# Long convolution with a gate: the first three transform stages on quarter blocks of the PE array

## The chip, the cores and the metric

One core of a Trainium2 chip. The metric is the device time of one execution in microseconds. Five engines are named as the profile names them: PE (the matmul array; PEld is its weight load), DVE (VectorE), ACT (ScalarE), POOL (GpSimd) and SP (SyncE, which issues the DMAs here). PSUM holds matmul results in banks of 512 fp32 columns on 128 partitions. All data are fp32.

## The reference, cut to what matters

```
x: (8, 6400, 128)   h: (6400, 128)                  # batch, time, channel
y = irfft(rfft(x, 12800) * rfft(h, 12800))[:, :6400]  # causal long convolution
gate = sigmoid(sum_k conv_w[k] * shift(y, 4 - k))     # 5 taps, causal
out = (gate * (y @ w_val)) @ w_out
```

## The kernel before, in words

The convolution is a shifted discrete Fourier transform of 6400 = 100 x 64 points, done as matmuls in four stages for one batch of 128 channels at a time. `n1`, `k1` run over 100 (`N1`), `n2`, `k2` over 64 (`N2`).

- Stage 1 (`Forward.group`, tile `x` or `h` to `gy` or `gh`): the weights loaded into the array are the data, 100 rows (`n1`) by 128 columns (two channels by 64 `n2`); the moving operand is the table `r1_sb` of 100 x 200 (cosines, sines). Four calls make a group of 8 channels, and 16 groups (`NG`) a batch. Four copies of 64 partitions x 400 columns bring a group from PSUM to `gy`, real part on partitions 0 to 63, imaginary on 64 to 127.
- Stage 2 (`s2_mm`): for each of the 100 `k1` one call with a 128 x 128 table (`m2_sb`) as weights and 128 channels moving, 8 values of `k1` to a step `kb`, 13 steps (`NKB`). `Product` multiplies by the spectrum of `h`: `swap` (ACT) copies the result from PSUM into `w` with the halves of the partitions exchanged, `mul_u` and `mul_t` (DVE) multiply, `add` (POOL) adds into `gy`. The spectrum is kept in DRAM (`hd`) as two tiles a step, each with its 64 rows doubled, and is loaded for every batch (`h_load`).
- Stage 3 (`s3_quad`): per channel one call, weights from `gy` (128 rows, 100 columns), the table `r3_sb` (128 x 128) moving; four channels fill a bank, which one copy of 100 x 512 brings to `dt`.
- Stage 4 (`Chunk.s4`): weights from `dt` (100 rows, 128 columns), the table `m4_sb` (100 x 100) moving, two calls for each of 64 time offsets. Then taps, projection, sigmoid, gate, output projection and store, in 13 chunks.

At the start the spectrum of `h` and the first batch are transformed. Then every batch has two phases. In phase A (`for g in range(NG)`) stage 3 of this batch runs beside stage 1 of the next one. In phase B (`for s in range(NCH)`) stage 4 and the gate of this batch run beside stage 2 and the product of the next. The last batch has no next one. In the profile phase A is for example 364 to 417 us and phase B 417 to 490 us. Every engine executes in the order in which the code is written (`_InOrder`). A PSUM `pair` is two banks, and two pairs take turns in the main loop; four single banks (`ps1`) serve stages 3 and 4.

Of the kernel before, what the change touches and what calls it, by code (L numbers as in the profile page):

```python
# [19 lines left out]
PX = 112  # L20
KB = 8
# [3 lines left out]
NG = C // XG  # L25
NW = 2 * C + TAPS
SW = 256
# [7 lines left out]
LATER = 5  # L35
M2B = 4
WB = 3
HB = 4
XB = 4
# [11 lines left out]
def _constants():  # L51
    k1 = np.arange(N1, dtype=np.float64)
    n1 = np.arange(N1, dtype=np.float64)
    k2 = np.arange(N2, dtype=np.float64)
    n2 = np.arange(N2, dtype=np.float64)
    tau = 2.0 * np.pi
    a = tau * np.outer(n1, k1 + 0.25) / N1
    r1 = np.concatenate([np.cos(a), -np.sin(a)], axis=1)
    al = tau * (
        (k1[None, :, None] + 0.25) * n2[:, None, None] / N  # L60
        + np.outer(n2, k2)[:, None, :] / N2
    )
    m2 = np.zeros((2, N2, N1, 2 * N2))
    m2[0, :, :, :N2] = np.cos(al)
    m2[1, :, :, :N2] = np.sin(al)
    m2[0, :, :, N2:] = -np.sin(al)
    m2[1, :, :, N2:] = np.cos(al)
    b = tau * np.outer(k2, n2) / N2
    r3 = np.zeros((2 * N2, N2, 2))
    r3[:N2, :, 0] = np.cos(b)  # L70
    r3[N2:, :, 0] = -np.sin(b)
    r3[:N2, :, 1] = -np.sin(b)
    r3[N2:, :, 1] = -np.cos(b)
    t = N2 * n1[None, :] + n2[:, None]
# [28 lines left out]
def longconv_moe(ctx: ExitStack, tc: tile.TileContext, x, h, r1, m2, r3, m4, w64, out):  # L103
# [98 lines left out]
    class Forward:  # L202


        def __init__(self, src, dst):
            self.src, self.dst, self.n, self.i = src, dst, 0, 0

        def load(self, n=1):
            for _ in range(n):
                if self.n < NG:  # L210
                    nc.sync.dma_start(x_sb[self.n % XB], self.src[self.n])
                    self.n += 1

        def group(self):
            g = self.i
            self.i += 1
            t = x_sb[g % XB]
            pt = pair()
            for m in range(4):
                nc.tensor.matmul(  # L220
                    pt[:, m // 2, (m % 2) * SW : (m % 2) * SW + 2 * N1],
                    lhsT=t[:N1, 2 * m : 2 * m + 2, :].rearrange("p j n -> p (j n)"),
                    rhs=r1_sb,
                    start=True,
                    stop=True,
                )
            self.load()
            v = pt.rearrange("p b (m x) -> p b x m", x=SW)
            return [
                lambda e, j=j, c=c: e(  # L230
                    self.dst[c * N2 : (c + 1) * N2, 4 * g + 2 * j : 4 * g + 2 * j + 2],
                    v[j * N2 : (j + 1) * N2, :, c * N1 : (c + 1) * N1],
                )
                for j in range(2)
                for c in range(2)
            ]

    def count(kb):
        return min(KB, N1 - kb * KB)

    def m2_load(kb):
        if kb < NKB:
            n = count(kb)
            nc.sync.dma_start(m2_sb[kb % M2B][:, :n], m2[:, kb * KB : kb * KB + n])

    def h_load(kb):
        if kb < NKB:
            n = count(kb) * C
            for r in range(2):
                nc.sync.dma_start(h_sb[(2 * kb + r) % HB][:, :n], hd[kb, r, :, :n])  # L250

    def h_double(kb):
        n = count(kb) * C
        for r in range(2):
            nc.sync.dma_start(hd[kb, r, N2:, :n], hd[kb, r, :N2, :n])

    def kdt(t, kb):
        n = count(kb)
        return t[:, : n * C].rearrange("p (d k t) -> p d k t", k=n, t=2)

    def s2_mm(src, kb):
        pt = pair()
        n = count(kb)
        for k in range(n):
            nc.tensor.matmul(
                pt[:, k // 4, (k % 4) * C : (k % 4 + 1) * C],
                lhsT=m2_sb[kb % M2B][:, k, :],
                rhs=src[:, :, kb * KB + k],
                start=True,
                stop=True,  # L270
            )
        if n <= 4:
            return pt[:, 0, : n * C].rearrange("p (k d t) -> p d k t", t=2, d=C // 2)
        return pt.rearrange("p b (k d t) -> p d (b k) t", t=2, d=C // 2)

    hx = h_sb + [dt[:, N1 * C + i * KB * C : N1 * C + (i + 1) * KB * C] for i in range(2)]

    class Spectrum:
        def __init__(self, kb):
            self.kb, self.v = kb, s2_mm(gh, kb)  # L280
            self.h = [hx[(2 * kb + r) % len(hx)] for r in range(2)]

        def real(self):
            t = kdt(self.h[0], self.kb)
            act(t[:N2], self.v[:N2])
# [392 lines left out]
```

## Time and profile before

| | |
|---|---|
| three runs | 1084.45, 1085.63, 1087.29 us (median 1085.63) |
| profiled execution, first to last instruction | 1083.8 us; a time of its own is not given beside this span |
| PE, PEld busy | 1048.2 us, 940.6 us |
| DVE, ACT, POOL busy | 848.5, 726.3, 407.5 us |
| DMA | 221.13 MB, mean 204 GB/s |

In the rows of groups "pt<-r_sb,x" is stage 1, "pt<-gy,m" stage 2, "pt<-r_sb,gy" stage 3, "pt<-m_sb,dt" stage 4; "128*100" are rows and columns of the loaded weights, then the output's partitions x columns and the moving operand's. All instructions carry the line of a helper, so tiles tell them apart. One matmul call of the program is recorded as two weight loads and two matmuls (two passes): stage 1 has 576 calls and 1152 of each. The profile's matmul durations include the way through the array, so they overlap.

### The profile page before, as it was taken

How to read it: one execution, taken by the hardware profiler on the slowest of the kernel's cores; microseconds unless marked ns; L12 is line 12 of the kernel's file. 1: busy time of each engine (PE TensorE's matmuls, PEld its weight loads, DVE VectorE, ACT ScalarE, POOL GpSimd, SP SyncE). 2: the span in 40 equal slices, each digit the busy share in tenths (PEclk: the TensorE clock that was granted, in tenths of full speed). 3: DMA queues.
4: the chain of work that ended last, by engine and by line, in shares of the span. 5: the costliest groups of instructions: out<-in, count | busy, mean ns of one | idle time of the engine just before them, and what ended most of it. 6: DMA issues, size and time to landing. Idle time of an engine off the chain costs nothing.

```text
span 1083.8 us, 19535 instructions
## 1 busy us (share of the span) xinstructions
PE 1048.2 (97%) x7480; PEld 940.6 (87%) x7480; DVE 848.5 (78%) x1180; ACT 726.3 (67%) x1176; POOL 407.5 (38%) x216
## 2 busy tenths in 40 slices
PE   8997899999999999999999999999999999999997
PEld 8997899779988899879998799888998789987975
DVE  5789778987599857987589866998579885998375
ACT  5799348865588556875488545984578645885365
POOL 0079005840078102870058400881028600683032
PEclk9999899999999999999999999999999999999999
DMA  5688957974199734977179742997249761892012
GB/s 149 216 305 202 363 181 257 305 227 166 53 336 274 263 94 145 333 214 243 53 271 309 232 151 67 333 280 255 77 172 322 215 228 51 291 309 78 18 38 84
DMA packets 109130, 221.13 MB, mean 204 GB/s; under 512 B 45354, under 2 KB 53518, under 8 KB 108814
## 3 DMA queue, kind: packets, MB, share of 16 engines
q1 hardware_dynamic: 109038, 219.89, 62.9%
q8 instruction: 59, 0.97, 0.4%
q14 instruction: 33, 0.27, 0.1%
HBM read 184.47 MB, written 39.32 MB: 206 GB/s over the span
## 4 chain that ended last, share of the span: by engine, by line
PE 79%; DVE 7%; ACT 6%; DMA 4%; issue 2%; POOL 1%; POOLq 0%; SPq 0%; DVEq 0%; ACTq 0%
PE pt L90 79%; DVE gl L90 2%; ACT w L90 2%; DVE w L90 2%; ACT dt L90 2%; DVE gy L90 2%; DMA x<-xl 1%; DMA h<-hd 1%; DMA m<-m 1%; ACT p L90 1%; DVE dt L90 1%; ACT gl L90 0%; DMA out<-yl 0%; ACT yl L90 0%; POOL gy L90 0%
## 5 line engine op out<-in xcount | busy, mean ns | idle before, releaser
L90 PEld LDWEIGHTS pt<-m_sb,dt 100*128 100x128 f32 x2048 | 242.4, 192 | 43.5 <-issue 30.1
L90 PEld LDWEIGHTS pt<-r_sb,gy 128*100 128x100 f32 x2048 | 239.6, 172 | 28.3 <-issue 24.6
L90 ACT COPY dt<-pt 100x512 f32<-100x512 f32 (+3 forms) x280 | 163.4, 584 | 137.0 <-PE pt L90 135.5
L90 PE MATMUL pt<-r_sb,gy 128*100 128x128 f32 x2048 | 244.7, 274 | 7.0 <-DVE gy L90 7.0
L90 POOL TENSOR_TENSOR gy<-gy,w 128x1024 f32<-128x1024 f32 x95 | 225.8, 2376 | 60.0 <-DVE w L90 59.4
L90 PE MATMUL pt<-m_sb,dt 100*128 100x100 f32 x2048 | 243.7, 274 | 3.5 <-DVE dt L90 2.6
L90 PE MATMUL pt<-r_sb,x 100*128 100x200 f32 x1152 | 216.4, 335 | 5.3 <-DMA x<-hl 4.3
L90 PEld LDWEIGHTS pt<-gy,m 128*128 128x128 f32 x1600 | 194.4, 188 | 24.0 <-issue 10.3
L90 DVE COPY dt<-pt 100x512 f32<-100x512 f32 (+2 forms) x165 | 112.2, 683 | 119.8 <-PE pt L90 117.9
L90 PE MATMUL pt<-gy,m 128*128 128x128 f32 x1600 | 201.7, 279 | 2.8 <-DVE dt L90 2.4
L90 PEld LDWEIGHTS pt<-r_sb,x 100*128 100x128 f32 x1152 | 193.1, 192 | 5.9 <-issue 5.3
L90 ACT COPY gy<-pt 64x400 f32<-64x400 f32 x256 | 124.6, 487 | 100.9 <-PE pt L90 88.6
L90 DVE COPY gy<-pt 64x400 f32<-64x400 f32 x256 | 146.4, 572 | 36.1 <-PE pt L90 33.5
L90 POOL MEMSET dt<- 128x4 f32 x8 | 0.8, 106 | 458.0 <-PE pt L90 458.0
L90 DVE TENSOR_TENSOR w<-w,h 128x1024 f32<-128x1024 f32 (+1 forms) x100 | 148.5, 1485 | 0.0
L90 DVE SCALAR_TENSOR_TENSOR dt<-pt,w_sb,dt 128x500 f32<-128x500 f32 (+7 forms) x216 | 132.5, 629 | 11.5 <-POOL dt L90 6.1
L90 ACT ACTIVATE w<-pt 64x1024 f32<-64x1024 f32 (+1 forms) x104 | 102.8, 989 | 38.3 <-PE pt L90 36.4
L90 DVE TENSOR_TENSOR gy<-pt,h 128x1024 f32<-128x1024 f32 (+1 forms) x100 | 117.5, 1175 | 12.1 <-ACT w L90 6.5
L90 POOL TENSOR_TENSOR dt<-dt,p 128x500 f32<-128x500 f32 (+1 forms) x64 | 101.5, 1586 | 58.0 <-DVE dt L90 34.9
L90 PE MATMUL pt<-dt,w_sb 128*128 128x500 f32 (+2 forms) x240 | 113.8, 564 | 2.3 <-ACT dt L90 2.3
L90 DVE SCALAR_TENSOR_TENSOR gl<-pt,w_sb,gl 128x500 f32<-128x500 f32 (+3 forms) x119 | 73.9, 622 | 38.9 <-ACT gl L90 29.8
L90 ACT COPY w<-pt 64x1024 f32<-64x1024 f32 (+1 forms) x104 | 101.1, 972 | 1.5
(35 smaller groups left out, 722.2 us busy)
## 6 DMA issues: line engine op xcount, KB each, us to landing
h<-hd SPq DMA_DIRECT2D x168, 512.0 KB, 6.8
m<-m SPq DMA_DIRECT2D x96, 512.0 KB, 6.5
x<-xl SPq DMA_DIRECT2D x128, 224.0 KB, 3.4
out<-dt SPq DMA_DIRECT2D x56, 250.0 KB, 6.0
out<-yl SPq DMA_DIRECT2D x40, 250.0 KB, 2.9
hd<-h SPq DMA_DIRECT2D x8, 512.0 KB, 5.7
x<-hl SPq DMA_DIRECT2D x16, 224.0 KB, 2.6
hd<-hd SPq DMA_DIRECT2D x14, 256.0 KB, 4.8
```

The lines of the kernel that those rows point to most:

```text
L90: return self._tc.keep_in_program_order(call(*args, **kwargs))
```

## The change

Stage 1 first folds the 100 values of `n1` in half: `sums` forms the sum (DVE) and the difference (POOL) of a row and its mirror image, 50 rows each, for 16 channels at a time. `half` multiplies these by tables of 50 x 100. Stages 1 and 3 then call the array in blocks of 64 rows x 64 columns, four calls on the four blocks in turn; stage 2 in blocks of 128 rows x 64 columns, two in turn. Calls rise from 3740 to 11240: stage 1 from 576 to 2304, stage 2 from 900 to 3600, stage 3 from 1024 to 4096. Stage 4 keeps its 1024 calls, with 128 rows of weights instead of 100.

In stage 2 the real part stands in one PSUM bank and the imaginary in the next, on all 128 partitions, so `swap` falls away: `mul_u` and `mul_t` read PSUM, each as two operations of 128 x 512, and `add` is two of 128 x 512. The spectrum needs one tile a step instead of two. Copies out of stage 1 go from four of 64 x 400 per 8 channels to two of 128 x 400. Loads of `x` go from 16 of 224 KB to 8 of 512 KB a batch, into two buffers (`XB`) instead of four; at the start six more buffers lie in `m4_sb`.

PE in phase A before, one group of eight channels and the start of the next (pt: PSUM tile, r_sb: table, gy and x: weights; rows are output partitions x columns, x4 means four calls):

```order
L90 MATMUL pt_1755<-r_sb,gy 100x128 x4
L90 MATMUL pt_1760<-r_sb,gy 100x128 x4
L90 MATMUL pt_1765<-r_sb,x_87 128x200 x4
L90 MATMUL pt_1784<-r_sb,gy 100x128 x4
L90 MATMUL pt_1789<-r_sb,gy 100x128 x4
```

and the same place now, from the end of stage 3 for eight channels into stage 1 (r_sb,x and r_sb,d alternate sixteen times, six shown):

```order
L96 MATMUL pt_3684<-r_sb,gy 64x128 x2
L96 MATMUL pt_3685<-r_sb,gy 64x128 x2
L96 MATMUL pt_3684<-r_sb,gy 50x128 x2
L96 MATMUL pt_3685<-r_sb,gy 50x128 x2
L96 MATMUL pt_3718<-r_sb,x_87 64x100
L96 MATMUL pt_3718<-r_sb,d_89 64x100
L96 MATMUL pt_3718<-r_sb,x_87 64x100
L96 MATMUL pt_3718<-r_sb,d_89 64x100
L96 MATMUL pt_3718<-r_sb,x_87 64x100
L96 MATMUL pt_3718<-r_sb,d_89 64x100
```

Eight plus four calls have become 32 plus 16, and two banks of stage 3 are filled at the same time.

DVE in phase B before, two steps (gy<-pt,h is `mul_u`, w<-w,h is `mul_t`, dt<-pt,w_sb,dt the taps, dt<-pt,dt the gate):

```order
L90 TENSOR_TENSOR gy<-pt_2258,h_83 128x64x16
L90 SCALAR_TENSOR_TENSOR dt<-pt_2270,w_sb,dt 128x5x100 x3
L90 TENSOR_TENSOR w_92<-w_92,h_84 128x1024
L90 TENSOR_TENSOR dt<-pt_2309,dt 128x5x100
L90 TENSOR_TENSOR gy<-pt_2299,h_85 128x64x16
L90 SCALAR_TENSOR_TENSOR dt<-pt_2311,w_sb,dt 128x5x100 x3
L90 TENSOR_TENSOR w_93<-w_93,h_86 128x1024
```

and now:

```order
L96 TENSOR_TENSOR gy<-pt_6416,h_84 128x64x8 x2
L96 SCALAR_TENSOR_TENSOR dt<-pt_6452,w_sb,dt 128x5x100 x3
L96 TENSOR_TENSOR w_91<-pt_6416,h_84 128x512 x2
L96 TENSOR_TENSOR dt<-pt_6515,dt 128x5x100
L96 TENSOR_TENSOR gy<-pt_6481,h_85 128x64x8 x2
L96 SCALAR_TENSOR_TENSOR dt<-pt_6517,w_sb,dt 128x5x100 x3
L96 TENSOR_TENSOR w_92<-pt_6481,h_85 128x512 x2
```

`mul_t` now reads the PSUM tile too, behind the taps, so the pair comes free there and no longer with `mul_u` and ACT's copies.

The diff, cut to its core (the tables of constants, the layout of `x` and `h` and the declarations of tiles that only follow from it are left out):

```diff
-XB = 4
+XB = 2
-HB = 4
+HB = 3
...
-        def group(self):
-            g = self.i
+        def sums(self):
+            j = self.i // 2
+            x, d = self.xs[j % len(self.xs)], d_sb[j % 2]
+            nc.gpsimd.tensor_tensor(out=d, in0=x[:, 0], in1=x[:, 1], op=ALU.subtract)
+            nc.vector.tensor_tensor(out=x[:, 0], in0=x[:, 0], in1=x[:, 1], op=ADD)
+
+        def half(self):
+            j, q = self.i // 2, self.i % 2
             self.i += 1
-            t = x_sb[g % XB]
+            x, d = self.xs[j % len(self.xs)], d_sb[j % 2]
             pt = pair()
             for m in range(4):
-                nc.tensor.matmul(
-                    pt[:, m // 2, (m % 2) * SW : (m % 2) * SW + 2 * N1],
-                    lhsT=t[:N1, 2 * m : 2 * m + 2, :].rearrange("p j n -> p (j n)"),
-                    rhs=r1_sb,
...
-            self.load()
+                for r, c in ((0, 0), (1, 1), (1, 0), (0, 1)):
+                    rows = slice(r * HP, r * HP + HR)
+                    nc.tensor.matmul(
+                        pt[c * N2 : (c + 1) * N2, r, m * N1 : (m + 1) * N1],
+                        lhsT=(d if c else x[:, 0])[rows, 4 * q + m, :],
+                        rhs=r1_sb[rows, c, :],
...
+            if q:
+                self.load()
...
     def s2_mm(src, kb):
...
-        for k in range(n):
-            nc.tensor.matmul(
-                pt[:, k // 4, (k % 4) * C : (k % 4 + 1) * C],
-                lhsT=m2_sb[kb % M2B][:, k, :],
-                rhs=src[:, :, kb * KB + k],
+        for s in range(n):
+            for c in range(2):
+                for p, k in ((0, 0), (1, 0), (1, 1), (0, 1)):
+                    o = (p + k) % 2
+                    nc.tensor.matmul(
+                        v[o * N2 : (o + 1) * N2, c, k * C // 4 : (k + 1) * C // 4, s, :],
+                        lhsT=m2_sb[kb % M2B][:, s, p, c * N2 : (c + 1) * N2],
+                        rhs=src[:, k * C // 4 : (k + 1) * C // 4, p * HR + kb * SB + s, :],
...
-        def swap(self):
-            nc.scalar.activation(self.t[:N2], self.v[N2:], AF.Copy, scale=-1.0)
-            act(self.t[N2:], self.v[:N2])
         def mul_u(self):
-            nc.vector.tensor_tensor(out=self.u, in0=self.v, in1=self.h[0], op=MUL)
+            for c in range(2):
+                nc.vector.tensor_tensor(out=self.u[:, c], in0=self.v[:, c], in1=self.h[:, 0], op=MUL)
         def mul_t(self):
-            nc.vector.tensor_tensor(out=self.t, in0=self.t, in1=self.h[1], op=MUL)
+            for c in range(2):
+                nc.vector.tensor_tensor(out=self.t[:, c], in0=self.v[:, c], in1=self.h[:, 1], op=MUL)
...
+        def add(self, e=nc.gpsimd):
+            for c, op in ((0, ALU.subtract), (1, ADD)):
+                e.tensor_tensor(out=self.u[:, c], in0=self.u[:, c], in1=self.t[:, 1 - c], op=op)
...
+    def s3_quads(d0):
+        pts = [single(), single()]
         for q in range(4):
-            d = d0 + q
-            nc.tensor.matmul(
-                pt[:N1, q * 2 * N2 : (q + 1) * 2 * N2],
-                lhsT=gy[:, d // 2, :, d % 2],
-                rhs=r3_sb,
+            for c in range(2):
+                for r, k in ((0, 0), (1, 0), (1, 1), (0, 1)):
+                    d, o = k * HP + d0 + q, (r + k) % 2
+                    m = HR if c else HP
+                    nc.tensor.matmul(
+                        pts[k][o * HP : o * HP + m, q * 2 * N2 : (q + 1) * 2 * N2],
+                        lhsT=gy[r * HP : (r + 1) * HP, d // 2, c * HR : c * HR + m, d % 2],
+                        rhs=r3_sb[r * HP : (r + 1) * HP, c, :],
+                        start=c == 0,
+                        stop=c == 1,
...
+        for g in range(NQ):
+            if nxt and g % 2 == 0:
+                fx.sums()
+            e = s3_quads(4 * g)
+            f = fx.half() if nxt else []
             e[0](act)
             e[1](dve)
-            for i in f:
-                i(act if g % 2 else dve)
+            if nxt:
+                f[0](act)
+                f[1](dve)
```

More of the change, by code (lines that the diff above doesn't have):

```diff
@@ L55, in _constants @@
     n2 = np.arange(N2, dtype=np.float64)
+    half = np.arange(2 * HP) % HP
+    own = half < HR
     tau = 2.0 * np.pi
-    a = tau * np.outer(n1, k1 + 0.25) / N1
-    r1 = np.concatenate([np.cos(a), -np.sin(a)], axis=1)
+    a = tau * np.outer(half + 0.5, k1 + 0.25) / N1
+    r1 = np.stack([np.cos(a) + np.sin(a), np.cos(a) - np.sin(a)], axis=1) * own[:, None, None]
     al = tau * (
@@ L243, in m2_load, with laid @@
             n = count(kb)
[L244 removed]
+            nc.sync.dma_start(m2_sb[kb % M2B][:, :n], m2[:, kb * SB : kb * SB + n])
     def h_load(kb):
         if kb < NKB:
[L248 to L257, printed above, removed]
+            n = 2 * count(kb) * C
+            nc.sync.dma_start(h_sb[kb % HB][:, :n], hd[kb, :, :n])
+    def laid(t, kb):
         n = count(kb)
[L259 removed]
+        return t[:, : 2 * n * C].rearrange("p (c d k t) -> p c d k t", c=2, k=n, t=2)
     def s2_mm(src, kb):
@@ L466, in longconv_moe @@
     wgen = weights()
-    fh, fx = Forward(h, gh), Forward(x[0], gy)
+    xh = x_sb + [
+        m4_sb.rearrange("p n t -> p (n t)")[:, i * 2 * XG * N2 : (i + 1) * 2 * XG * N2].rearrange(
+            "p (a d n) -> p a d n", a=2, n=N2
+        )
+        for i in range(6)
+    ]
+    fh, fx = Forward(h, gh, xh), Forward(x[0], gy, xh)
     nc.sync.dma_start(r1_sb, r1)
-    fh.load(XB)
+    fh.load(NS)
     for f in (fh, fx):
-        for g in range(NG):
-            e = f.group()
-            if f is fh and fh.n == NG:
-                left = fx.n - (g + 1 - (NG - XB))
-                if left < 0:
-                    fx.load(-left)
-            for i in e:
-                i(act if g % 2 else dve)
+        for g in range(NQ):
+            if g % 2 == 0:
+                f.sums()
+            e = f.half()
+            if f is fh and g % 2:
+                fx.load()
+            e[0](act)
+            e[1](act if g % 2 else dve)
         if f is fh:
@@ L491, in longconv_moe @@
         if kb + 1 < NKB:
-            sp[kb + 1].real()
+            sp[kb + 1].copy()
+            sp[kb + 1].store()
         if 0 <= kb < NKB:
-            pr[kb].swap()
-        if kb >= 1:
-            pr[kb - 1].mul_u()
-            pr[kb - 1].mul_t()
-            if kb < NKB - 1:
-                pr[kb - 1].add()
-        if kb + 1 < NKB:
-            sp[kb + 1].imag()
-            sp[kb + 1].store()
-    for d in (slice(0, C // 4), slice(C // 4, C // 2)):
-        for kb in (NKB - 2, NKB - 1):
-            pr[kb].add(nc.vector, d)
+            pr[kb].mul_u()
+            pr[kb].mul_t()
+            pr[kb].add(nc.vector if kb == NKB - 1 else nc.gpsimd)
     pairs.pop([p is ps2 for p in pairs].index(False))
```

174 lines of the change are left out of this document (75 added, 99 removed).

## The prediction

> **What bounds the kernel now.** First the page's busy times, then the stretches of the phases (columns: PE, PEld, DVE, ACT, POOL busy, PE clock, DMA share, GB/s).
>
> ```profile
> PE 1048.2 (97%) x7480; PEld 940.6 (87%) x7480; DVE 848.5 (78%) x1180; ACT 726.3 (67%) x1176; POOL 407.5 (38%) x216
> ```
> ```profile
> 0.00:52.00 52.00, 47.33 (x268) 47.09 (x269) 36.62 (x64) 31.60 (x64) 0.20 (x4) 1.00 0.60 178
> 52.00:112.00 60.00, 47.96 (x391) 46.90 (x391) 52.23 (x42) 52.68 (x56) 44.65 (x22) 0.91 0.84 257
> 364.00:417.00 53.00, 52.87 (x384) 49.78 (x383) 36.52 (x59) 26.63 (x53) 0.00 (x0) 1.00 0.42 144
> 417.00:490.00 73.00, 72.01 (x519) 61.89 (x518) 64.07 (x80) 58.55 (x88) 49.60 (x25) 1.00 0.84 264
> ```
>
> PE is busy 52.9 of 53 us in phase A and 72.0 of 73 in phase B. Only around the spectrum (52 to 112 us) do ACT and DVE hold the pace, with 52 of 60 us each. So the sum is one over matmul passes. Their spacing comes from the timeline, because durations overlap.
>
> ```profile
> 364.35 1.91 PE L90 MATMUL pt<-r_sb,gy 128*100 128x128 f32 x16
> 366.10 1.52 PE L90 MATMUL pt<-r_sb,x 100*128 100x200 f32 x8
> 437.64 2.37 PE L90 MATMUL pt<-m_sb,dt 100*128 100x100 f32 x20
> 440.75 2.04 PE L90 MATMUL pt<-gy,m 128*128 128x128 f32 x16
> ```
> ```profile
> L90 PE MATMUL pt<-r_sb,gy 128*100 128x128 f32 x2048 | 244.7, 274 | 7.0 <-DVE gy L90 7.0
> L90 PE MATMUL pt<-m_sb,dt 100*128 100x100 f32 x2048 | 243.7, 274 | 3.5 <-DVE dt L90 2.6
> L90 PE MATMUL pt<-r_sb,x 100*128 100x200 f32 x1152 | 216.4, 335 | 5.3 <-DMA x<-hl 4.3 <-DMA x<-xl 0.5 <-DVE gl L90 0.5
> L90 PE MATMUL pt<-gy,m 128*128 128x128 f32 x1600 | 201.7, 279 | 2.8 <-DVE dt L90 2.4 <-DVE gy L90 0.2
> ```
>
> A burst less its last duration, over its steps, is the spacing: stage 3 (1.91 - 0.274)/15 = 109 ns, stage 1 (1.52 - 0.335)/7 = 169, stage 2 (2.04 - 0.279)/15 = 117, stage 4 (2.37 - 0.274)/19 = 110. Stage 3 against stage 1 gives (169 - 109)/72 = 0.83 ns a moving column. Stage 4 moves 100 columns, which would be 86 ns, but loads 128 weight columns, and stands at 110: there the weight load sets the pace, 0.86 ns a weight column. With 1152, 2048, 2048 and 1600 + 200 passes the four stages take 195, 223, 225 and 211 us of PE.
>
> **The change part by part.** The price that decides is not in this trace: every call here takes the whole array, and none shows how many calls on different blocks run at a time. Call that number k. Two blocks of stage 2 and four of stages 1 and 3 are named, so k lies between 1 and 2, and 1 and 4.
>
> Stage 1: 2304 calls are 4608 passes of 100 columns, 86 ns by the slope. At k = 4 that is 99 us instead of 195; at k = 1, 396. Per g in phase A it is 8 x 86 = 0.69 us instead of 8 x 169 = 1.35: 16 x 0.66 = 10.6 a batch, 75 over seven. At the start PE would need only 32 x 0.69 = 22 us of the 52, but 16 loads of 512 KB are 8.4 MB, at the 257 GB/s of the next stretch 33 us: 19 saved there.
>
> Stage 2: 7200 passes of 64 columns. The slope gives 109 - 64 x 0.83 = 56, half of stage 2's own spacing 58; I take 57. At k = 2 that is 205 us against 211, nothing in the sum; at k = 1, 410.
>
> Stage 3: 8192 passes of 128 columns, as the contraction is halved and the outputs too: 223 us at k = 4, as before; 446 at 2; 893 at 1.
>
> I take full overlap, k = 4 and 2, because of what the rows show of the array: a pass lasts 274 ns and the next begins 109 ns later, so more than one is in flight, and a weight load of 110 ns lies under the matmul before it. I assume that a block waits for nothing but its own earlier pass; the other ends become rivals.
>
> [...]
>
> Change of block shape: 255 places in program order, 26 in each of the first phases B. The trace has no such change. Bounds: nothing (stage 4 follows projections without a gap), or the way through the array, 274 - 109 = 165 ns each, 42 us. Nearer to neither: half, 20 us. [...]
>
> The vector engines:
>
> ```profile
> L90 DVE COPY gy<-pt 64x400 f32<-64x400 f32 x256 | 146.4, 572 | 36.1 <-PE pt L90 33.5
> L90 ACT COPY gy<-pt 64x400 f32<-64x400 f32 x256 | 124.6, 487 | 100.9 <-PE pt L90 88.6 <-DVE gl L90 10.1
> L90 DVE TENSOR_TENSOR w<-w,h 128x1024 f32<-128x1024 f32 x92 | 127.6, 1387 | 0.0
> L90 DVE TENSOR_TENSOR gy<-pt,h 128x1024 f32<-128x1024 f32 x92 | 112.0, 1218 | 12.1 <-ACT w L90 6.5 <-DMA h<-hd 4.9 <-ACT dt L90 0.6
> L90 DVE TENSOR_TENSOR gy<-pt,h 128x512 f32<-128x512 f32 x8 | 5.4, 680 | 0.0
> L90 ACT ACTIVATE w<-pt 64x1024 f32<-64x1024 f32 x96 | 98.1, 1022 | 38.2 <-PE pt L90 36.4 <-POOL dt L90 0.6
> L90 ACT COPY w<-pt 64x1024 f32<-64x1024 f32 x96 | 96.4, 1005 | 1.4
> L90 POOL TENSOR_TENSOR gy<-gy,w 128x1024 f32<-128x1024 f32 x95 | 225.8, 2376 | 60.0 <-DVE w L90 59.4
> L90 POOL TENSOR_TENSOR dt<-dt,p 128x500 f32<-128x500 f32 x40 | 78.7, 1968 | 34.4 <-DVE dt L90 24.9 <-PE pt L90 4.9 <-ACT dt L90 4.6
> ```
>
> ACT loses 1.02 + 1.01 us a step, 26 us a batch, and with DVE half of the 64 copies a batch of stage 1 (17 us in all, since 128 partitions take as long as 64). DVE's product is 4 x 0.68 = 2.72 us instead of 2.61, and it gains eight sums of about 0.68. All this lies beside PE, so it counts for nothing there. Around the spectrum it does count: ACT falls to 26 x 0.6, DVE to about 40 us, and the 60 us fall to PE's 26 products, 26 x 32 x 57 ns = 47 us, and a ramp of 4: 9 saved. POOL's add of 512 columns costs half of 2.38, or as the 500 columns 1.97. At 1.2 POOL has 13 x 2.4 a batch as before; at 1.97 it has 26 x 1.97 + (49.6 - 13 x 2.38) = 70 us, just inside phase B. I take the former, the same two tiles, and nothing in the sum.
>
> `mul_t` behind the taps frees the pair. DVE has 64 + 1.5 of 73 us in phase B, so it runs under a step behind; bounds 0 and 0.5 us for each of 91 steps, the idle share spread on the steps. I take 0.1: 9 us.
>
> The loads of `x`:
>
> ```profile
> h<-hd SPq DMA_DIRECT2D x168, 512.0 KB, 6.8
> m<-m SPq DMA_DIRECT2D x96, 512.0 KB, 6.5
> x<-xl SPq DMA_DIRECT2D x128, 224.0 KB, 3.4
> ```
>
> With two buffers a load waits for the second half of 16 channels and must be followed by POOL's difference (1.2 to 2.0) and DVE's sum (0.7, in place, so behind POOL). With 2.43 us per g at k = 4, four g's are 9.7 us; the loop is load + 2.3 + two halves and a stage 3 (3.1). It fits up to a load of 4.3 us. The rows bound the load by 3.4 (half the size) and 6.8 (same size, full DMA). At 6.8 it costs 2.5 us each four g's, 70 in all; at 3.4 nothing. Phase A moves 144 GB/s, so nearer to the first: 10 us. Spectrum loads fall from 168 of 512 KB to 84; their cover in phase B grows.
>
> Sum against the profiled execution: 1083.8 - 75 - 19 - 9 + 20 + 9 + 10 = 1020. The median of the runs is 1085.6, 1.8 over its span: 1022. Its own range, from all the small costs at nothing (983, rounded down) to the block shapes and DVE's pair at their upper and POOL's adds at some of theirs: 980 to 1085.
>
> **Rivals.** 1. Two at a time (slower). A call is two passes of the same block (1152 rows of stage 1 for 576 calls), and in every burst of the trace passes start one after another. If they must start in program order, the second pass of block one waits for its first, and block two's first starts only with it. Then four blocks overlap no more than two: stage 2 is still free, stage 1 costs 198 instead of 195, stage 3 446 instead of 223. Place: phase A, 16 x 1.77 = 28 us a batch and in the last one too. 1083.8 + 3 + 223 - 9 + 20 + 1.8 = 1323. Break-even: (396 + 893)/k must undercut 418 by the 30 us of small terms, k = 3.3; below it this rival decides. [...]
>
> 2. Weight loads in line. Stage 4 shows the load as the bound at 110 ns for 128 columns. If loads of different blocks don't overlap, 64 columns cost 55 ns whatever the block: stage 1 253 (+59), stage 2 396 (+185), stage 3 at two at a time (+223): 1573. Against it: nothing in the trace, as each load here covers all columns.
>
> 3. No overlap at all: stage 1 +201, stage 2 +200, stage 3 +670: about 2177.
>
> 4. Overlap is full but is given back: the load of `x` at 6.8 us (+60 on the sum) leaves 1082. It needs POOL's and DVE's parts in line behind the load, which the order shows.
>
> **How the numbers follow.** Full overlap 0.44, rival 4 0.10, rival 1 0.26, rival 2 0.14, rival 3 0.06. Predicted 1022. The range from 980 to 1395 takes in full overlap, rivals 4 and 1 with the block shapes at 42 us and DVE's pair at 45 (1323 + 22 + 45 and some), 0.80 of the chance. Within 0.3% (3 us, about what a measurement of this kernel can tell from no change) lies little but half of rival 4: 0.06. Faster 0.44 + 0.03 = 0.47, slower 0.47.
>
> **What would show it.** Stage 3's spacing per pass in a burst: 27 ns for full overlap, 54 for rival 1, 109 for rival 3; stage 2's 28 or 55; stage 1's 21, 43 or 86. Phase A 44 us (81 by rival 1), phase B about 76. PE waiting for POOL's d or DVE's x in phase A would be rival 4; PE waiting for DVE's w in phase B, a pair that is freed late. The prediction is wrong if k in stage 3 is under 3.3.

## The result, and the profile after

The change makes the kernel slower: 1112.5 us (median of four runs, 1111.6 to 1116.8) against 1086.5 (1084.5 to 1087.7), a ratio of 1.0246 with a 95% interval of 1.0223 to 1.0268. The profiled execution has a span of 1111.3 us, 27.5 more than before. PE is busy nearly as long as before:

```profile
PE 1036.4 (93%) x22480; PEld 879.9 (79%) x22480; DVE 770.2 (69%) x1278; ACT 442.1 (40%) x838; POOL 447.3 (40%) x388
```

Yet each block of the array runs as was forecast. The timeline of PE (start, length, engine, operation, count) shows a burst of stage 2 and one of stage 4 in phase B, and in phase A one of stage 3 and the first rounds of one of stage 1:

```profile
365.97 1.16 PE L96 MATMUL pt<-gy,m 128*64 128x64 f32 x32
...
368.01 2.37 PE L96 MATMUL pt<-m_sb,dt 128*128 128x100 f32 x20
...
375.92 1.98 PE L96 MATMUL pt<-r_sb,gy 64*64 64x128 f32 x64
377.72 0.25 PE L96 MATMUL pt<-r_sb,x 50*64 50x100 f32 x1
...
377.81 0.24 PE L96 MATMUL pt<-r_sb,x 50*64 50x100 f32 x1
...
377.90 0.24 PE L96 MATMUL pt<-r_sb,x 50*64 50x100 f32 x1
```

The 64 passes of stage 3, each recorded as 0.275 us long, stand (1.98 - 0.275)/63 = 27 ns apart (109 before for a whole-array pass). Stage 1 starts a round of four blocks every 86 ns, 21.5 ns a pass. In stage 2 the spacing within a burst is 29.2 ns, where the forecast has 57 over two blocks. The time is lost between the bursts. The phases (span of each, from the first pass of stage 3 or 4 to the next, the last one to PE's last pass) show where:

| stretch | before | after | difference |
|---|---|---|---|
| start, to the first pass of stage 2 | 50.7 | 63.7 | +13.0 |
| spectrum and first product | 61.1 | 56.4 | -4.7 |
| phase A, first | 51.5 | 55.8 | +4.3 |
| phases A, six middle ones | 54.9 to 55.6 | 52.7 to 54.7 | -7.8 in all |
| phases B, seven | 70.6 to 72.0 | 73.4 to 73.5 | +18.3 in all |
| last phase A (stage 3 alone) | 35.1 | 39.4 | +4.4 |
| last phase B | 55.4 | 55.4 | 0 |

Stretches of the kernel after (start, spectrum, first phase A, a middle A, a B, the last A; columns as in the prediction):

```profile
0.00:63.70 63.70, 47.07 (x1026) 42.64 (x1026) 19.97 (x32) 22.47 (x47) 22.02 (x20) 1.00 0.51 175
63.70:120.10 56.40, 49.72 (x1604) 49.37 (x1602) 31.73 (x54) 14.43 (x28) 29.43 (x24) 0.96 0.69 219
120.10:175.90 55.80, 46.38 (x1537) 42.36 (x1537) 33.64 (x62) 16.78 (x31) 11.23 (x9) 0.94 0.54 184
375.90:428.60 52.70, 49.16 (x1549) 41.90 (x1549) 33.53 (x51) 21.22 (x41) 8.76 (x7) 1.00 0.46 157
428.60:502.10 73.50, 73.05 (x1098) 60.74 (x1098) 61.22 (x106) 30.06 (x57) 45.41 (x41) 1.00 0.60 173
1012.70:1052.10 39.40, 36.39 (x1037) 30.17 (x1037) 19.09 (x28) 13.68 (x25) 0.00 (x0) 1.00 0.10 35
```

Phase B is full as before. Phase A was full too:

```profile
361.20:416.10 54.90, 54.79 (x397) 51.64 (x396) 37.21 (x60) 27.38 (x54) 0.00 (x0) 1.00 0.45 150
```

Now PE idles 3.5 to 9.4 us in it although no other engine is busy for more than 34 us of it. The waits of PE name the cause only in part (us in total, times, longest):

```profile
PE pt L96 <- issue: 33.9, 46, 2.2
PE pt L96 <- DVE x L96: 17.8, 10, 8.8
```

"Issue" means that PE waited for nothing that the profile shows. Before the change PE has no wait of this kind. The page has one more line that changed, the queue that carries PE's own instructions (packets, MB); before and after:

```profile
q8 instruction: 59, 0.97, 0.4%
```
```profile
q8 instruction: 177, 2.90, 1.1%
```

2.90 MB in 177 packets are 16 KB each. PE executes two weight loads and two passes for a call, and with some 300 that only handle semaphores these come to 45,273 instructions in the trace (15,293 before), so a packet holds 256. Laid along that list, the passes of the trace show that, behind the start, nearly nine tenths (88%) of the excess of gaps over 200 ns inside a stage fall on the same 8 of 256 places, the start of such a block. And these stalls end with the packets: of 42 over 0.3 us at block starts, 37 end 1.2 to 1.8 us after a packet has landed, one packet to a block and always the next of the row. These stalls sum to 12.1 us in the first phase A, 3.3 to 5.9 in the others, 2.4 in the last, and to nothing before the change. Phase A now takes 192 instructions of PE per 2.43 us; before it took 48 per 3.1.

So PE's instructions come in blocks of 256, a packet of q8 to each, and the starts of these blocks cost 43 us in the eight phases A.

### The profile page after: what moved, and what is told of

It is laid out like the page before. It is cut to its first block, busy times and chain, and to the rows that moved or that the text cites. A ratio compares the mean times of both kernels' runs of the same rounds, so it can differ in the third digit from the quotient of the medians.

```text
span 1111.3 us, 49204 instructions
## 1 busy us (share of the span) xinstructions
PE 1036.4 (93%) x22480; PEld 879.9 (79%) x22480; DVE 770.2 (69%) x1278; ACT 442.1 (40%) x838; POOL 447.3 (40%) x388
## 4 chain that ended last, share of the span: by engine, by line
PE 82%; DVE 7%; issue 4%; DMA 3%; ACT 2%; POOL 1%; POOLq 0%; SPq 0%; ACTq 0%; DVEq 0%
PE pt L96 82%; DMA x<-xl 3%; DVE gl L96 2%; DVE gy L96 2%; DVE w L96 2%; DVE dt L96 1%; ACT dt L96 1%; POOL d L96 1%; ACT gl L96 1%; DVE x L96 1%; ACT yl L96 0%; DMA x<-hl 0%; POOL dt L96 0%; POOLq L669 0%; ACT p L96 0%
## 5 line engine op out<-in xcount | busy, mean ns | idle before, releaser
L96 PE MATMUL pt<-r_sb,gy 64*64 64x128 f32 (+1 forms) x8192 | 268.1, 274 | 24.0 <-issue 17.9
L96 PEld LDWEIGHTS pt<-r_sb,gy 64*64 64x64 f32 (+1 forms) x8192 | 235.9, 130 | 66.9 <-issue 40.8
L96 POOL TENSOR_TENSOR gy<-gy,w 128x512 f32<-128x512 f32 (+1 forms) x206 | 251.0, 1243 | 76.1 <-DVE w L96 75.5
L96 PEld LDWEIGHTS pt<-m_sb,dt 128*128 128x128 f32 x2048 | 242.8, 192 | 43.0 <-issue 36.0
L96 ACT COPY dt<-pt 128x512 f32<-128x512 f32 (+2 forms) x276 | 157.4, 576 | 248.6 <-PE pt L96 238.7
L96 PE MATMUL pt<-m_sb,dt 128*128 128x100 f32 x2048 | 244.9, 275 | 3.8 <-DVE dt L96 3.8
L96 PEld LDWEIGHTS pt<-gy,m 128*64 128x64 f32 x6400 | 196.9, 136 | 38.6 <-PE pt L96 30.7
L96 PE MATMUL pt<-gy,m 128*64 128x64 f32 x6400 | 209.1, 222 | 3.1 <-DVE w L96 1.9
L96 DVE SCALAR_TENSOR_TENSOR dt<-pt,w_sb,dt 128x500 f32<-128x500 f32 (+7 forms) x216 | 132.9, 631 | 34.6 <-issue 17.8
L96 PE MATMUL pt<-r_sb,d 50*64 50x100 f32 x2304 | 151.5, 277 | 2.9 <-issue 2.7
L96 PE MATMUL pt<-r_sb,x 50*64 50x100 f32 x1920 | 117.0, 257 | 23.5 <-DVE x L96 17.8
L96 PEld LDWEIGHTS pt<-r_sb,d 50*64 50x64 f32 x2304 | 131.9, 154 | 3.7 <-issue 3.7
L96 PEld LDWEIGHTS pt<-r_sb,x 50*64 50x64 f32 x1920 | 101.4, 140 | 32.5 <-DVE x L96 20.4
L96 DVE SCALAR_TENSOR_TENSOR gl<-pt,w_sb,gl 128x500 f32<-128x500 f32 (+3 forms) x119 | 74.0, 623 | 44.6 <-ACT gl L96 21.9
```

Of the source, the lines that this page charges most:

```text
L96: return self._tc.keep_in_program_order(call(*args, **kwargs))
```

## The experiments

Theories: F, PE gets its instructions too late for 192 per 2.43 us; X, the loop of loads, differences and sums holds phase A. All kernels ran beside the kernel before on the same chip; ratios are to it.

**1. No sums** (`a_nosums`).

```diff
-            nc.gpsimd.tensor_tensor(out=d, in0=x[:, 0], in1=x[:, 1], op=ALU.subtract)
-            nc.vector.tensor_tensor(out=x[:, 0], in0=x[:, 0], in1=x[:, 1], op=ADD)
...
-                        lhsT=(d if c else x[:, 0])[rows, 4 * q + m, :],
+                        lhsT=x[rows, c, 4 * q + m, :],
```

> The changed kernel without sums and differences: stage 1 takes the two raw halves of the loaded tile, so the fold is left out of the computation; PE's calls, their number and order stay as they are. Theory F (PE's own instructions are fetched too late: 192 of them per 2.43 us of work in phase A, and PE stands at the starts of 256-instruction blocks): middle phases A (53 to 55 us) lose at most the waits that end with x or d, about 2.5 us each, so 51 to 52, and the start (120 us to the first phase A) loses a little; total 1112 - 15 to -25. Theory X (the loop of loads, difference and sum holds phase A): middle phases A fall to 45 or 46; total about 1112 - 65.

Measured: 1095.9 us, ratio 1.0081 (1.0060 to 1.0102). Middle phases A 52.2 to 54.4, as with the sums; PE's waits for x were gone and the stalls at block starts grew to 5.4 to 7.8 us a phase. X falls: what the loop gives back, the instruction supply takes. The start fell by 20 us (first stage 2 at 44.0 instead of 63.7), far more than I had allowed it, so the sums do hold the start. The stretch behind it gave 6.8 us of that back (63.2 instead of 56.4), with 8.9 us of stalls at block starts.

**2. Stage 1 in blocks of 64 x 128** (`a_s1wide`).

```diff
-            for m in range(4):
-                for r, c in ((0, 0), (1, 1), (1, 0), (0, 1)):
+            for m in range(0, 4, 2):
+                for c in range(2):
+                    for r in range(2):
...
-                        lhsT=(d if c else x[:, 0])[rows, 4 * q + m, :],
+                        lhsT=(d if c else x[:, 0])[rows, 4 * q + m : 4 * q + m + 2, :].rearrange("p j n -> p (j n)"),
```

> The changed kernel with stage 1 in blocks of 64 rows x 128 columns, two channels a call: half as many calls of stage 1 on twice the columns, so the same time on the array (its outputs stand in another layout, so the result is not the reference's). PE's instructions per g fall from 192 to 160 in the stream of stage 1 and 3 (64 less 32 of stage 1), while the array's work, the loads, the sums and the copies stay. Theory F: phase A goes by instructions, 160/192 of about 53 is 44 at best; 48 to 50 us each, total 1112 - 20 to -35. Theory X: phases A unchanged at 53 to 55 us, total within 5 us of 1112.

Measured: 1131.8 us, ratio 1.0410 (1.0389 to 1.0431), middle phases A 55.5 to 56.6. Both expectations missed, since the array's work didn't stay: a pass took 57.8 ns instead of two times 21.5, and stages 1 and 3 now had different block shapes. 199 ns lay between the last pass of stage 3 and the first of stage 1, 201 on the way back, where 27 and 58 would do without a change of shape: up to 16 x (172 + 143) = 5 us a phase. The stalls at block starts fell to about 1 us, as F says for fewer instructions, but the run doesn't separate the theories by its time.

**3. Both copies of a half on one engine** (`a_onecopy`).

```diff
-            e[0](act)
-            e[1](act if g % 2 else dve)
+            for i in e:
+                i(act if g % 2 else dve)
```

> The changed kernel with both copies of a half of stage 1 on one engine, ACT for odd and DVE for even ones, as the kernel before has it, instead of one copy on each. At the start the two copies of one tile go one after another (0.49 on ACT, then 0.57 on DVE), with DVE's sum behind the second and PE behind the sum. If this chain sets the 3.47 us per 16 channels, then with alternate engines the start falls from 120.1 us to the first phase A to 105 or 110; if the loads set it (my forecast's 33 us) or PE's instructions, it stays at 118 to 120. Phases A and B unchanged by either, so total 1098 to 1102 or 1110.

Measured: 1116.9 us, ratio 1.0279 (1.0236 to 1.0322); the first phase A began at 119.3 us. The order of the copies is not the cause. The ring of the start closes with one engine as well; DVE there:

```profile
40.66 1.06 DVE L96 COPY gy<-pt 128x400 f32<-128x400 f32 x2 [1.77 <-PE pt L96]
41.63 0.68 DVE L96 TENSOR_TENSOR m_sb<-m_sb 128x512 f32<-128x512 f32 x1
44.08 1.05 DVE L96 COPY gy<-pt 128x400 f32<-128x400 f32 x2 [1.77 <-PE pt L96]
45.05 0.68 DVE L96 TENSOR_TENSOR m_sb<-m_sb 128x512 f32<-128x512 f32 x1
```

The sum for the next 16 channels (41.63) stands behind the copies of this half, PE behind the sum, the next copies behind PE's first half: 1.06 + 0.68 + 1.77 less the overlap = 3.42 us a turn, 16 turns.

**4. A mixture** (`h1`): stage 1 as changed (its difference in place), all else as before, so 96 instructions per g for about the same array time.

```diff
+            nc.gpsimd.tensor_tensor(out=x[:, 1], in0=x[:, 0], in1=x[:, 1], op=ALU.subtract)
+            nc.vector.scalar_tensor_tensor(out=x[:, 0], in0=x[:, 0], scalar=2.0, in1=x[:, 1], op0=MUL, op1=ALU.subtract)
...
         for g in range(NG):
-            e = [s3_quad(8 * g), s3_quad(8 * g + 4)]
+            if nxt and g % 2 == 0:
+                fx.sums()
+            e = [s3_quad(4 * g), s3_quad(64 + 4 * g)]
-            f = fx.group() if nxt else []
+            f = fx.half() if nxt else []
```

> A mixture: stage 1 folded and in blocks of 64 x 64 as in the changed kernel (difference written in place, so no further buffer; both copies of a half on one engine), and stages 2, 3 and 4, product and spectrum as in the kernel before (whole-array calls). Per g of eight channels stage 3 has 16 instructions of matmul and as many loads instead of 64 and 64, stage 1 the same 32 and 32 as the changed kernel: 96 instead of 192 instructions for the same 2.43 us of array time. Theory F: phases A near their array time of 44 plus two block changes a g, 45 to 48 us against 54.9 before and 53.5 in the changed kernel; total 1010 to 1035, faster than the kernel before. Theory X: the loop of loads and sums is the same, so phases A stay at 52 to 54, total 1070 or more.

Measured: 1100.4 us, ratio 1.0120 (1.0078 to 1.0162). The stalls at block starts are gone (0.1 to 0.3 us a middle phase A), as F says, but the phases took 51.9 to 54.1, as X said. The trace divides that up: 14 of 16 changes from stage 3 to stage 1 took 202 ns (109 without one), all changes back 176 (21 without), which is 4.0 us a phase; two others waited 3.0 us for x (`PE <- DVE x`); and the start was even longer, 67.1 us.

**5. Sums one step of 16 channels ahead** (`a_ahead`, on the changed kernel).

```diff
-XB = 2
+XB = 3
...
-            if nxt and g % 2 == 0:
-                fx.sums()
+            if nxt and g % 2 == 0:
+                if g == 0:
+                    fx.sums()
+                fx.sums()
```

> The changed kernel with sums and differences formed one step of 16 channels ahead (the difference in place, so that a third x buffer fits where the d tiles were). In the changed kernel every step of the start is a ring of 3.47 us: sum, PE's two halves, copies, next sum; and PE's passes stand 41.6 ns apart there, 21.4 in phase A. Theory R (the ring sets the start, and a PE that waits in each ring stays at half pace): the ring opens, PE's passes go at about 21 ns for most of the start, which is then bound by loads: first stage 2 at 42 to 47 us instead of 63.7, as without any sums (44.0). Rival (half pace belongs to the start whatever PE does): 32 halves x 1.33 + ramp of 8 = 51 us. Phases A: theory F (late instructions) says 52 to 53.5 (only the 2 to 4 us a phase that wait for x go, and most come back as stalls at block starts); theory X says 46 to 48. Total 1088 to 1094 by R and F, 1045 to 1055 with X.

Measured: 1095.0 us, ratio 1.0070 (1.0044 to 1.0095). First stage 2 at 47.5 us, 16.1 earlier; middle phases A 51.0 to 53.4, stalls at block starts 4.3 to 7.0 (the first phase A took 56.2, 13.1 of it in such stalls). R and F, not X, though not by the loads that R names (see the start below). In the changed kernel PE's rounds of four passes in the start stand 167 ns apart:

```profile
29.78 0.37 PE L96 MATMUL pt<-r_sb,m_sb 50*64 50x100 f32 x1
...
29.95 0.37 PE L96 MATMUL pt<-r_sb,m_sb 50*64 50x100 f32 x1
...
30.11 0.37 PE L96 MATMUL pt<-r_sb,m_sb 50*64 50x100 f32 x1
```

That is half the pace of phase A (86 ns above), throughout 8 to 62 us. The row of the start has a clock of 1.00 above, but the trace holds no record of the granted clock before 64.8 us, and where it has none the row counts it as full. With the sums ahead the first record stands at 13.5 us, and most of the start goes at 21.5 ns a pass. The stretches of start and a middle phase A of this kernel, and two pieces of its start:

```profile
0.00:47.50 47.50, 29.64 (x1024) 28.11 (x1024) 24.88 (x31) 21.73 (x47) 24.11 (x20) 0.93 0.68 234
361.00:413.80 52.80, 48.93 (x1549) 42.31 (x1549) 34.35 (x51) 21.19 (x41) 9.10 (x7) 1.00 0.42 146
13.60:37.00 23.40, 15.19 (x617) 13.74 (x609) 16.15 (x20) 12.90 (x30) 16.04 (x11) 1.00 0.83 267
37.40:44.00 6.60, 6.19 (x148) 6.19 (x152) 2.35 (x4) 2.76 (x6) 0.00 (x0) 0.50 0.13 49
```

The same 1024 passes keep PE busy for 29.6 us instead of 47.1. In the piece at a clock of 1.00 a pass takes 21.5 ns, in the one at 0.50 41.8: there the half pace is the granted clock. The passes ahead of the first record stand as far apart, so I take it to be the clock there as well. Here the first record comes 4.7 us after the first pass; the start of the changed kernel, in which PE is busy for 47.07 of 63.7 us with a pause in every ring of 3.47 us, keeps the half pace until 62 us. What raises the clock isn't shown beyond that.

**6. Stage 3 with half the columns** (`a_s3half`).

```diff
-                        rhs=r3_sb[r * HP : (r + 1) * HP, c, :],
-                        start=c == 0,
-                        stop=c == 1,
+                        rhs=r3_sb[r * HP : (r + 1) * HP, c, :N2],
+                        start=True,
+                        stop=True,
```

> The changed kernel with stage 3 moving 64 columns of its table in each call instead of 128 (half of stage 3 is left out: the two parts of a contraction are not added, and half of the columns is missing). The number of PE's instructions, their order and blocks stay; the array's time per pass falls from 27.2 to about 14 or 16 ns (weight load of 64 columns 55 ns over four blocks), so 16 x 64 x 12 = 12 us a phase A. Theory F (PE gets its instructions too late): at 192 instructions in what would be 1.7 us, PE waits at block starts for most of what it saves: phases A of 53.5 fall by 0 to 5 us, the last one (39.5, with 128 instructions per 1.8 us) by 2 to 8. Theory S (only array time, block changes and waits for x count, stalls at block starts are a symptom): phases A fall by 9 to 12 us to about 43, the last one to 28. Total 1112 - 35 or less by F, 1112 - 75 to -95 by S.

Measured: 1099.1 us, ratio 1.0109 (1.0070 to 1.0148). A middle phase A and the last one:

```profile
374.30:424.90 50.60, 38.60 (x1550) 31.43 (x1549) 32.81 (x51) 20.82 (x41) 8.70 (x7) 0.97 0.48 163
1004.70:1038.20 33.50, 25.70 (x1037) 20.06 (x1037) 19.03 (x28) 13.57 (x25) 0.00 (x0) 0.95 0.12 41
```

A pass fell from 27.2 to 15.1 ns, 12.4 us a phase. The middle phases fell only from 53.8 to 52.3 on average, PE idle 12 us of 51, and the stalls at block starts rose to 7 to 13.5 us. The last one fell by 5.9 of 12.4. A part of what didn't come is the granted clock, which was lower in these phases (0.97 in the rows of three middle phases, 0.93, 0.85 and 0.88 in the others); but the three at 0.97, where that is worth under 2 us, took 50.6 to 52.1. This decides for F: phase A is set by how fast PE's instructions come, not by the array.

**7. Grouped mixture, sums ahead** (`h3a`).

```diff
-        for g in range(NG):
-            e = [s3_quad(4 * g), s3_quad(64 + 4 * g)]
-            f = fx.half() if nxt else []
+        for j in range(NS):
+            e = [s3_quad(8 * j + d) for d in (0, 64, 4, 68)]
+            f = [fx.half(), fx.half()] if nxt else []
...
+            if nxt:
+                fx.sums()
+            for g in (2 * j, 2 * j + 1):
+                if trail:
+                    trail.pop(0)()
```

> The mixture (stage 1 folded and in blocks of 64 x 64, the rest with whole-array calls) with stage 3 of 16 channels ahead of both halves of stage 1, so half as many changes of block shape, and with sums and differences one step ahead. Theory: in the mixture a change from whole array to blocks costs 400 - 109 = 291 ns and one back 176 - 21 = 155, 16 of each a phase A = 7.1 us, two thirds of the 10.6 us that stage 1 saves. With 8 of each, phases A fall from 54.0 to 50 or 51; waits for x would go too. The start falls from 67.1 to 43 to 47 us at the first stage 2 if its ring sets it (before: 50.7). Phases B 71.4 as in the mixture (70.65 before). Total 1050 to 1062, faster than the kernel before by 2 to 3.5%. If the changes of shape don't matter and the loop of x does, phases A stay at 52 to 54 and the total is 1070 to 1080.

Measured: 1096.1 us, ratio 1.0074 (1.0048 to 1.0099). The first phase A took 44.6 us (51.5 before, 55.8 in the changed kernel): with half the instructions and no stalls most of stage 1's saving is there, 6.9 of 10.6 us, and eight pairs of changes of shape take 2.0 of the rest. Both totals of the expectation were missed. The price of a change of shape that this expectation used was wrong, for 400 ns was a mean with two waits in it; 93 + 155 ns a pair is right. The middle phases took 54.8 to 57.7, because two pieces of the last chunks' work stood together at the end of a step:

```profile
109.20:153.80 44.60, 44.55 (x768) 42.26 (x768) 31.16 (x64) 15.59 (x30) 8.68 (x7) 0.93 0.86 306
354.90:409.70 54.80, 48.78 (x782) 43.04 (x780) 32.08 (x52) 19.67 (x39) 7.81 (x6) 0.97 0.44 154
```
```profile
PE pt L98 <- DVE gl L98: 3.2, 2, 1.7
PE pt L98 <- ACT dt L98: 2.8, 1, 2.8
```

**8. Trailing work spread** (`h3b`).

```diff
-            for g in (2 * j, 2 * j + 1):
-                if trail:
-                    trail.pop(0)()
+            if trail:
+                trail.pop(0)()
```

> The grouped mixture with the trailing work of the last chunks (taps, projection, sigmoid, gate, store) spread one piece to each step of 16 channels, the late chunks' four taps in two pieces, instead of two pieces together at the end of a step. In the grouped mixture the first phase A, which has no trailing work, took 44.6 us (51.5 before), and the others 54.8 to 57.7, where PE stood up to 2.8 us behind DVE's four taps of 0.74 in a row. Theory: this pile of DVE's is all that separates them, and the instruction stream is no limit at 96 per g; then the middle phases A take 44.6 + 6 projections (about 5.5) = 49 to 51 and the last one 35 to 36; total 1096 - 6 x 5.5 - 2 = 1055 to 1068, faster than the kernel before by 2 to 3%. Theory F alone, if PE's instructions come late here too, leaves them at 54 or more and the total at 1085 or more.

Measured: 1061.3 us, ratio 0.9767 (0.9728 to 0.9807), middle phases A 51.2 to 52.7 (a little above 51), the last 33.0, with the phase B behind it 2.7 us longer. What was left is one wait, for a sum whose x stood behind the transfers for phase B:

```profile
PE pt L98 <- DVE x L98: 3.3, 1, 3.3
```

**9. One load of stage 4's table** (`a_m4once`, on `a_ahead`): the 16 loads of the first phase A in one. It asks why that phase has 12 us of stalls.

```diff
-                m4_load(4 * g, 4 * g + 4)
+                if g == 0:
+                    m4_load(0, N2)
```

> The changed kernel with the sums one step ahead, and the table of stage 4 loaded in one transfer at the start of the first phase A instead of 16 of 205 KB, one in each g. In the changed kernel PE's stalls at the starts of instruction blocks take 12 to 13 us in the first phase A and 4 to 7 in the later ones. If the 16 transfers between the loads of x delay PE's instructions, the first phase A falls from 56.2 to 50 or less; if not, it stays at 55 to 57 (or loses a little at its beginning, beside one transfer of 3.3 MB). No other phase changes by more than 1 us.

Measured: one run, 1093.9 us; the first phase A 56.25 us, 12.8 of it in stalls. The 16 small transfers are not the cause.

**10. Transfers for phase B spread** (`a_spread` on `a_ahead`, `h3c` on `h3b`).

```diff
-            for kb in range(M2B):
-                m2_load(kb)
-            for kb in range(HB):
-                h_load(kb)
+            pre = [lambda kb=kb: m2_load(kb) for kb in range(M2B)] + [lambda kb=kb: h_load(kb) for kb in range(HB)]
...
+                if g % 2 and g > 1 and pre:
+                    pre.pop(0)()
```

> The changed kernel with the sums one step ahead, and the seven transfers of 512 KB for the next phase B (four of m, three of h) issued one in every second g instead of all at the start of phase A. There the DMA engines stand at 405 to 410 GB/s for the first 12 us of phase A, and PE's 256-instruction blocks last 4.5 to 7 us, against 3.3 to 3.6 late in the phase, where hardly anything is moved (their array time is 3.25). Theory C (instructions come late because their fetch stands beside these transfers): phases A of 51 to 53.5 fall to 47 to 49, blocks to 3.3 to 4 throughout; total 1095 - 20 to -30, 1065 to 1075. Theory F without C (192 instructions per 2.43 us are too many for the fetch whatever else is moved): the stalls only spread out, phases A 51 to 53, total 1090 to 1095.

> The grouped mixture with spread trailing work, and the transfers for the next phase B (four of m, two pairs of h) issued one to each step of 16 channels from the second on, instead of all at the start of phase A. There PE waited 3.1 to 3.3 us in each middle phase A for a sum whose x stood behind these transfers. Theory: this wait goes, phases A of 51.2 to 52.7 take 47.5 to 49, total 1061 - 17 to -22 = 1039 to 1045. If the wait only moves (x behind later transfers, or phase B waiting for m), phases A or B keep it, total 1055 to 1062.

Measured: `a_spread` 1106.8 us, ratio 1.0184 (1.0153 to 1.0215), phases A 51.8 to 58.8: slower than either theory had it. Its longest stall, on PE's timeline:

```profile
406.39 1.48 PE L96 MATMUL pt<-r_sb,gy 64*64 64x128 f32 x48
411.10 0.69 PE L96 MATMUL pt<-r_sb,gy 64*64 64x128 f32 x8 [3.23 <-issue]
```

and the packets of PE's instructions around it, from the list of DMA packets:

```
start us   took us   bytes
398.26     0.91      16384
401.72     1.26      16384
408.73     0.99      16384
412.34     1.04      16384
```

The usual step between packets is 3.5 us; here it is 7.0, so one that was due at 405.2 came at 408.7. The rate of all transfers from 401 to 413 us, in slices of 0.31 us:

```profile
GB/s 0 0 55 27 27 164 109 382 410 410 219 123 137 137 205 287 341 382 396 410 396 423 437 437 410 478 410 396 396 369 273 109 41 27 27 27 0 55 0 0
```

The late packet moved amid 380 to 480 GB/s of data (the 18th to the 29th slice), and the stall ended 1.4 us after it had landed (the 0.35 us in the expectation of experiment 11 was misread). That suggests that transfers hold up the fetch, and that spreading them only brought more blocks beside one; experiment 11 asks it directly. (I had also read blocks of 4.5 to 7 us early in a phase as late; most of them hold the projections.)

`h3c` took 1040.85 us, ratio 0.9572 (0.9552 to 0.9591): 4.3% faster than the kernel before, and so faster than both. All six middle phases A took 46.4 us, and PE waits for nothing in them. That is the forecast of stage 1 come true: 54.9 less 10.6, and 2.0 for eight pairs of changes. It is a little better than expected here because in `h3b` the granted clock had fallen behind the wait (0.94 over the phase with that wait), and now stays at 1.00:

```profile
107.10:160.30 53.20, 44.52 (x768) 41.93 (x769) 31.29 (x64) 16.46 (x32) 8.56 (x7) 0.92 0.79 269
355.40:401.80 46.40, 46.40 (x781) 41.83 (x780) 31.28 (x51) 19.30 (x39) 7.67 (x6) 1.00 0.52 172
401.80:473.40 71.60, 69.75 (x500) 59.55 (x499) 65.28 (x80) 57.08 (x85) 52.94 (x27) 1.00 0.84 270
```

The first phase A lost by it (53.2 instead of 44.6 us), and so did the phase B behind it (75.7 instead of 72.7); a version that leaves that phase A as it was wasn't tried.

**11. No loads in phase A** (`a_noload`, on `a_ahead`).

```diff
-            if q:
+            if q and len(self.xs) > XB:
                 self.load()
...
-        if nxt:
-            for kb in range(M2B):
-                m2_load(kb)
-            for kb in range(HB):
-                h_load(kb)
```

> The changed kernel with the sums one step ahead, without the loads that run in phase A: the first three tiles of x of a batch are used again for its other five, and the first four tiles of m and three of h of phase B are those left over from the batch before (the transform is that of other data; the work of all engines stays). With the transfers spread, PE's longest stall in a phase A (3.5 us) ended 0.35 us after an instruction packet that began 7.0 us after the one before, when a burst of data at 400 to 440 GB/s had passed. Theory C (the packets wait behind data, and at 192 instructions per 2.43 us PE has used up the block before by then): without the data phases A of 51 to 53.5 fall to 45.5 to 48, with under 1.5 us of stalls at block starts. Theory F (the fetch is too slow for 192 instructions per 2.43 us with free DMA engines as well): 50 to 53. Total 1095 - 7 x 6 = 1050 to 1058 by C, 1085 to 1095 by F; the last phase A (39.5, no loads) and phases B as they were.

Measured: 1071.4 us, ratio 0.9835 (0.9796 to 0.9873), between the two. First and a middle phase A:

```profile
107.00:156.40 49.40, 44.79 (x1536) 42.07 (x1536) 34.27 (x62) 17.21 (x32) 11.70 (x9) 0.94 0.23 80
353.60:403.50 49.90, 47.58 (x1549) 41.63 (x1548) 35.99 (x51) 21.00 (x41) 9.88 (x7) 1.00 0.08 29
```

Stalls at block starts fell from 13.1 to 6.7 us in the first and from 4.3 to 7.0 to 1.4 to 2.6 us in the middle phases. So about half to two thirds of the lateness is data in front of the fetch; the rest remains with the DMA engines at 8% of their time, where a block of 256 lasts 3.2 us on the array. The trace shows how little room that leaves. In the middle phases A the packet for a block starts when PE has just begun the block before it: 1.1 us later in the changed kernel and 0.7 here (medians), and 1.3 us ahead in the kernel before, where a block lasts some 18 us. The packet takes 1.0 us in each, and a stalled PE goes on 1.4 us after the landing. By these figures a fetch comes to an estimated 3.5 us beside the loads and 3.1 without them, against the block's 3.2. What the 1.4 us consist of stays open.

## Why the prediction was wrong, point by point

The sum had 64 us less, and the span became 27.5 longer, 91.5 apart: 61.5 in the seven phases A (-75 + 10 against -3.5), 32 in the start, 4.3 around the spectrum, 4.4 in the last phase A, and 10.7 the other way in the phases B (20 + 9 against 18.3).

- **Full overlap, k = 4 and 2** was right: 27.2, 21.5 and 29.2 ns a pass, as forecast. Rivals 1 to 3 fell with it. That the measured time lies between 980 and 1395 is luck all the same: the range joins two distant mechanisms, 1022 and 1323, and neither of them gave 1112. Rival 1's strict order of starts doesn't show as a limit between different blocks here: stage 3 took 27.2 ns a pass, not 54.
- **"16 x 0.66 = 10.6 a batch, 75 over seven"** is the step that failed most. Array time did fall by that (10.6 x 7 is 74), but the seven phases A became 3.5 us shorter in all. I priced a call by its passes alone. Calls rise from 3740 to 11240, and the trace of before had a line for what carries them (59 packets on q8), which I did not read. Of the 72 us that are missing, 40 are stalls at block starts (12.1 + 3.3 + 4.9 + 5.9 + 5.0 + 5.1 + 4.0), 8.5 waits for x (17.8 in all less 9.3 in the start). Of the other 23, about 9 are changes of shape at the projections (36 pairs in the six middle phases, 93 + 155 ns each) and at most 5 the granted clock (0.94 in the row of the first phase, 0.97 in one other); the rest are gaps that I didn't single out. Experiments 1 and 6 show that taking one of these away doesn't free the phase: the instructions come no faster.
- **"The start ... 33 us ... 19 saved"** came out as +13. It took the loads as the bound. PE, copies and sum form a ring of 3.47 us in program order (experiment 3), and the PE that waits in it ran at half pace (41.8 ns a pass, 21.5 for most of the start with the ring open; experiment 5). With the ring open the start takes 47.5 us, and it is not the loads of x that fill it: PE waits 8.8 us for the first sum and 7.8 us as "issue" (5.3 of it at once, from 32.5 us, beside 300 to 400 GB/s of data), and goes at half pace up to 13.5 us and again from 37.3 to 44.2. 234 GB/s x 47.5 us = 11.1 MB are moved in it, 2.7 more than the h and x that I counted, for the first tables are loaded there too.
- **Spectrum, 9 saved:** 4.7 measured. ACT and DVE left the path as said; PE's own time in it is near the forecast, but this stretch, too, is rich in instructions (12 blocks in 56 us), and two stalls at block starts, at 95 and 109 us, take 3.5 us.
- **Changes of shape (+20) and the late pair (+9):** the first was about right, the second was small. Phases B gained 18.3 us. From a projection's pass to the first of stage 2 it is 512 ns (419 before), from stage 4 to stage 2 205 (112), so 93 ns for this change; from stage 2 to either 150, where its own pass takes 29, so 121 for the change back: between the half of 165 that I took and its whole. Eleven such pairs in a phase B (22 changes, not the 26 that I had counted) are 2.4 of the 2.6 us that it grew by. PE waited only 1.9 us for DVE's `w`, so the late pair cost at most that of its 9.
- **The loop of x (+10, rival 4)** was real but small: 8.5 us in phases A, and hidden behind the instructions once these are late. With few instructions (`h3b`) it shows as 3.3 us a phase, and goes when the transfers ahead of it are moved (`h3c`).
- **The last phase A** (+4.4) wasn't in the sum: stage 3 alone, with 2.4 us at block starts and most of the rest at changes of shape.
- The working of `mul_u`, `mul_t` and `add` was right (DVE 682 and 681 ns an operation of 512 columns, POOL 1.28 us; a copy of 128 x 400 took 0.49 us on ACT and 0.57 on DVE, as one of 64 x 400 did before), and mattered nowhere.

## What to carry to other kernels

Splitting calls over blocks of the array made each cheaper for the array (27 ns a pass of stage 3 instead of 109) and not for the instruction stream (59 packets of PE's instructions became 177): work out PE's instructions per microsecond, and treat 192 in 2.4 us as past what arrives in time beside data transfers and 96 in 2.4 us as safe, on what this kernel shows (a block of 256 lasts 3.2 and 6.5 us then, and its fetch about 3.5). Split the stage that the array's shape wastes (stage 1, where the fold halves the passes) and leave the others whole, and group the calls of one shape, since each pair of changes cost 0.25 us here (93 + 155 ns). Before a phase is called bound by loads, follow program order around one turn of it; a sum that stood one step too late in its engine's order set the pace of all engines in the start here (63.7 us, 47.5 with the sums ahead).

## What the runs showed of the hardware that I had not expected

- PE's stalls for its own instructions, up to 2.4 us each in the changed kernel, whose PE is 93% busy, and 5.3 in the start of experiment 5; the profile books most of them as "issue".
- Such a stall could cost twice: after two of them, 2.1 and 2.2 us long, the granted clock of the changed kernel was at half for 3.4 us, from 518.8 and from 95.5 us.
- The half pace of PE while it waits in each turn of a ring (41.8 ns a pass against 21.5). Spacings show it; the row of the clock doesn't, since it reads 1.00 where the trace has no record yet.
- Four blocks of 64 x 64 in turn, two passes and two weight loads a call, overlapped fully: 27.2 ns a pass of stage 3, where one of the whole array took 109. A change from the whole array to blocks cost 93 ns, one back 155 in `h1` and 121 from stage 2 of the changed kernel.
